# Moving half of one input tile to the weight ring, and one ScalarE copy ahead of a scaling

## The chip, the cores and the metric

The kernel runs on one core of one Trainium2 chip. The metric is the device time of one execution in microseconds, from the first to the last instruction of the core with what surrounds them; the profile's own span is a little shorter (131.2 us of an execution of 132.94 us). Before the change the median of three runs is 132.91 us (132.47 to 132.97).

## The reference

Two stages are computed. The first is a state-space scan over 4 batches x 8 heads, sequence 768, head size 32, state size 16. With `cum` the running sum of log a inside a chunk:

```
L   = exp(cum_i - cum_j), kept where i >= j
y   = ((C B^T) * L) x  +  (C state) * exp(cum_i)
state = exp(cum_last) * state + sum_j B_j x_j exp(cum_last - cum_j)
```

The second is a bilinear feed-forward layer over the 3072 tokens with 256 features: `out = ((y w_a) * (y w_b)) w_out`, with 1536 inner features. All inputs and the output are float32; the kernel multiplies in float16.

## The kernel before, in words

**Tiling.** The sequence is cut into 6 blocks of 128 steps, and two batches are worked on together. A "pair" p is one block of two batches, so there are 12 pairs. Each pair has three input tiles, B (`bn`), C (`cn`) and x (`xn`), and each tile is loaded in two halves, one for each batch (`bt` 0 and 1): `load1(eng, p, which, bt)`, with which = 0 for B, 1 for C, 2 for x. A half of B or C is 64 KB in runs of 128 bytes, a half of x 128 KB.

**Queues.** The engine named in `load1` issues the transfer: SyncE, ScalarE or GpSimd. Each issuer has a queue of its own (q1 SyncE, q10 ScalarE, q0 GpSimd) and the 16 DMA engines serve all of them. GpSimd's queue also carries the weights, converted to float16 on the way: `load_w(0)` and `load_w(1)` bring the first and second halves of w_a and w_b (`Wa`, `Wb`), `load_wo` brings w_out.

**Stages of a pair.** `scale_bc` multiplies B and C by the decay factors and gives `bm` and `cm` (L259). `transposes` turns these on PE (L286); copies bring them to `bt` (ScalarE, L297) and `ct` (DVE, L298). `scores` multiplies them on PE into the PSUM tiles SC0 and SC1 (L320). `mask` multiplies the scores with the causal mask (L354, DVE); with `by_pool=True`, ScalarE first copies the scores from PSUM to `tmp` (L351) and GpSimd multiplies (L352). `scale_x` scales x to float16 (`X16`, L243 on ScalarE). `pv_u` (L363) multiplies the masked scores with X16; the result goes to `X2T` (L451 on ScalarE, L453 on DVE for pair 0). `unit(p, k2)` is a piece of the feed-forward layer: the matmuls `aps` with Wa and `bps` with Wb (L504), a copy of `aps` on ScalarE (L518) and the product on DVE (L525). `out_mm` multiplies with w_out (L538).

**Order.** The order on each engine is written out by hand, and the engines run their own lists in that order, waiting on semaphores. Around the change it is: the loads and GpSimd's constants; pair 0 up to X2T, with `warmup` matmuls (L193) that only keep PE busy; then pair 1's C and B scaled (`scale_bc(1, 1, nc.vector)` on DVE and `scale_bc(1, 0, nc.gpsimd)`), its transposes, the first matmuls with Wa, the scores of pair 1, and so on. On DVE, `cm` of pair 1 stands ahead of the scan of block 2, of one of the four X2T evacuations of pair 0, and of the copy of the transposed C. Pair 2's x is made to wait for the second half of Wb. From pair 4 on, the transposes are done by DMA.

Of the kernel before, what the change touches and what calls it, by code (L numbers as in the profile page):

```python
# [22 lines left out]
def kernel(  # L23
# [13 lines left out]
    nc = tc.nc  # L37
# [85 lines left out]
    def load1(eng, p, which, bt, i0=0, n=64):  # L123
        blk, bp = divmod(p, NBP)
        src = (B, C, x)[which][2 * bp + bt, :, blk * Q + 2 * i0 : blk * Q + 2 * i0 + 2 * n, :]
        return eng.dma_start(  # L126
            pair_in[p][which][64 * bt + i0 : 64 * bt + i0 + n].rearrange("i h r n -> i h (r n)"),
            src.rearrange("h (i r) n -> i h (r n)", r=2),
        )
# [5 lines left out]
    def load_w(half):  # L135
        c = slice(half * KC, (half + 1) * KC)
        return [
            nc.gpsimd.dma_start(W[half], src.rearrange("(f p) e -> p f e", p=128)[:, :, c])
            for W, src in ((Wa, moe_w_a), (Wb, moe_w_b))
        ]  # L140
# [17 lines left out]
    load1(nc.scalar, 0, 2, 1)  # L158
    load1(nc.sync, 0, 2, 0)
    load1(nc.sync, 1, 0, 0)  # L160
    load1(nc.sync, 1, 1, 1)
    nc.sync.dma_start(c32, p32_t.ap())
    nc.vector.memset(warm.bitcast(u32), 0)  # L163
    nc.vector.memset(zero, 0.0)
# [19 lines left out]
        )  # L184
    load1(nc.gpsimd, 1, 0, 1)
    load1(nc.gpsimd, 1, 1, 0)
    load_w(0)
    for bt in range(2):
        load1(nc.gpsimd, 1, 2, bt)

    def warmup(n, bank, cols=512):
        for _ in range(n):
            nc.tensor.matmul(  # L193
                bank[:, 0:cols], warm[:, 0:128], warm[:, 0:cols], start=True, stop=True, skip_group_check=True
            )
# [42 lines left out]
    def scale_x(p, eng):  # L238
        X16 = mid.tile([128, H, 2, D], f16, name="x16", tag="x16")
        xo, xi = X16.rearrange("p h r d -> p (h r d)"), pair_in[p][2].rearrange("p h r d -> p (h r d)")  # L240
        st.setdefault(p, {})["X16"] = X16
        if eng is nc.scalar:
            nc.scalar.mul(xo, xi, XS)  # L243
        else:
            eng.tensor_scalar(xo, xi, XS, None, ALU.mult)  # L245
# [66 lines left out]
    def scores(p):  # L312
        BT, CT = st[p]["BT"], st[p]["CT"]
        for e in range(2):
            for r in range(2):
                for m in range(4):
                    for bt in range(2):
                        rows = slice(32 * m, 32 * m + 32)
                        c0 = (e * 2 + r) * Q
                        nc.tensor.matmul(  # L320
                            SC[m][64 * bt : 64 * bt + 64, c0 : c0 + Q],
                            BT[rows, e, r, bt],
                            CT[rows, bt],
                            start=True,
                            stop=True,
                            skip_group_check=True,
                            tile_position=(32 * m, 64 * bt),
                        )
        st[p]["T1"] = mid.tile([128, H, 2, Q], f16, name="t1", tag="t1")
# [8 lines left out]
    def product0(m2, e):  # L338

        return (  # L340
            st[0]["T1"][:, 4 * m2 : 4 * m2 + 4].rearrange("p (m e) r q -> p e m (r q)", e=2)[:, e],
            (SC0, SC1)[m2][:, :, e * 256 : e * 256 + 256],
        )

    def mask(out_in, by_pool=False, ri=False):
        o_, i_ = out_in
        c_ = causal_ri.rearrange("p r s i -> p (r s i)") if ri else causal.rearrange("p r q -> p (r q)")
        c_ = c_.unsqueeze(1).broadcast_to((128, 2, 2 * Q))
        if by_pool:
            tmp = mid.tile([128, 2, 2 * Q], f32, name="tmp", tag="tmp")  # L350
            nc.scalar.copy(tmp, i_)  # L351
            nc.gpsimd.tensor_tensor(out=o_, in0=tmp, in1=c_, op=ALU.mult)  # L352
        else:
            nc.vector.tensor_tensor(out=o_, in0=i_, in1=c_, op=ALU.mult)  # L354
# [237 lines left out]
    warmup(1, SC[3])  # L592
    warmup(2, SC[3], 128)
    scores(0)
    scale_x(0, nc.scalar)
    mask(product0(0, 0))
    mask(product0(0, 1))
    mask(product0(1, 1), by_pool=True)
    mask(product0(1, 0))
    warmup(3, tcp)  # L600
    scale_bc(1, 1, nc.vector)
# [202 lines left out]
```

## Time and profile before

| | before |
|---|---|
| time, median of 3 | 132.91 us |
| span of the profile | 131.2 us |
| mean granted PE clock | 0.974 |
| PE busy | 122.2 us (93%) |
| DVE busy | 88.6 us (68%) |
| ScalarE (ACT) busy | 72.6 us (55%) |
| GpSimd (POOL) busy | 55.7 us (42%) |
| chain that ended last | PE 85%, DMA 9%, the rest 6% |

The page divides the span into 40 slices and gives for each engine the busy share in tenths, and for PE the granted clock. The chain that ended last goes back from the last instruction to what released it, step by step. A group's line in the listings gives the source line, the engine, the operation, the tile written and read, and in brackets the idle time just ahead of it with its releaser. The DMA listing counts packets and bytes by queue.

### The profile page before, as it was taken

The page shows a single profiled execution, that of the slowest core. Times are in us where ns is not written, and L with a number is a line of the kernel's source. Part 1 is how long each engine was busy: PE and PEld are TensorE (multiplying, and loading weights), DVE is VectorE, ACT ScalarE, POOL GpSimd, SP SyncE. Part 2 cuts the span into 40 slices and gives each one's busy share as a digit, 9 for nine tenths or more (in the row PEclk, how much of TensorE's full clock was granted, in tenths as well). Part 3 has the DMA queues.
Part 4 walks back from the last instruction along what each step waited for, and adds up shares of the span by engine and source line. Part 5 has one row for each costly group of instructions (what it writes and reads, how often), then busy time and mean ns, then how long its engine had stood idle before and what let it go on. Part 6 is the DMA issues. An engine that isn't in the chain of part 4 may idle for free.

```text
span 131.2 us, 4785 instructions
## 1 busy us (share of the span) xinstructions
PE 122.2 (93%) x1964; PEld 102.5 (78%) x1964; DVE 88.6 (68%) x165; ACT 72.6 (55%) x144; POOL 55.7 (42%) x99
## 2 busy tenths in 40 slices
PE   6972599999999999999999999999999999999990
PEld 2531368898889898888888988988988888899990
DVE  2570657698597895894995985967957929925450
ACT  1460372579455647657548647566476576485530
POOL 7959049575975092290650923806437000000000
PEclk9999559999999999999999999999999999999999
DMA  3999948996314546634775566465565011110112
GB/s 71 169 159 222 168 93 162 173 202 111 84 50 90 95 127 116 168 73 66 179 70 95 157 110 140 105 102 146 97 127 143 5 45 40 40 40 5 40 40 80
DMA packets 45989, 13.79 MB, mean 105 GB/s; under 512 B 41008, under 2 KB 45776, under 8 KB 45968
## 3 DMA queue, kind: packets, MB, share of 16 engines
q1 hardware_dynamic: 42048, 10.12, 37.4%
q0 software_dynamic: 1920, 3.02, 13.4%
q10 hardware_dynamic: 2000, 0.36, 1.5%
q8 instruction: 15, 0.25, 0.8%
q14 instruction: 6, 0.05, 0.1%
HBM read 11.13 MB, written 3.15 MB: 109 GB/s over the span
## 4 chain that ended last, share of the span: by engine, by line
PE 85%; DMA 9%; ACT 1%; ACTq 1%; DVE 0%; issue 0%; DVEq 0%
PE aps L504 26%; PE ops L538 24%; PE bps L504 24%; DMA cn<-in_C_dram 9%; PE SC L320 3%; PE SC L363 3%; PE SC L380 1%; PE SC L425 1%; PE fps L221 1%; PE ops L759 1%; ACT bt L297 1%; ACTq L126 1%; PE SC L286 0%; ACT asb L518 0%; PE SC L397 0%; DVE cm L259 0%
## 5 line engine op out<-in xcount | busy, mean ns | idle before, releaser
L525 DVE TENSOR_TENSOR hk<-bps,asb 128x512 f16<-128x512 f32 x72 | 49.2, 687 | 17.9 <-ACT asb L518 17.6
L518 ACT COPY asb<-aps 128x512 f32<-128x512 f32 x72 | 42.1, 587 | 17.8 <-PE aps L504 16.7
L504 PE MATMUL aps<-X2T,Wa 128*128 128x256 f16 x288 | 44.6, 279 | 0.0
L504 PE MATMUL bps<-X2T,Wb 128*128 128x256 f16 x288 | 43.6, 276 | 0.0
L538 PE MATMUL ops<-Wo,hk 128*128 128x256 f16 x276 | 33.9, 273 | 0.0
L504 PEld LDWEIGHTS <-Wb 128*128 128x128 f16 x288 | 30.1, 105 | 2.2
L504 PEld LDWEIGHTS <-Wa 128*128 128x128 f16 x288 | 29.1, 105 | 3.4 <-DVE X2T L453 0.3
L538 PEld LDWEIGHTS <-hk 128*128 128x128 f16 x276 | 26.0, 98 | 3.6 <-DVE hk L525 0.2
L354 DVE TENSOR_TENSOR t<-SC,causal_ri 128x512 f16<-128x512 f32 x32 | 21.1, 681 | 0.0
L251 POOL TENSOR_TENSOR planes<-cn,fC 128x256 f16<-128x256 f32 x8 | 5.0, 620 | 32.2 <-DMA cn<-in_C_dram 22.8
L553 ACT ACTIVATE osb<-ops 128x256 f32<-128x256 f32 x23 | 8.8, 384 | 16.5 <-PE ops L538 16.3
L245 POOL TENSOR_SCALAR x<-xn 128x512 f16<-128x512 f32 x9 | 13.4, 1489 | 0.8
L441 ACT ACTIVATE X2T<-SC 64x256 f16<-64x256 f32 (+1 forms) x24 | 10.9, 456 | 4.9 <-PE SC L380 3.7
L354 DVE TENSOR_TENSOR t<-SC,causal 128x512 f16<-128x512 f32 x13 | 8.4, 683 | 1.8 <-PE SC L320 1.7
L468 DVE SCALAR_TENSOR_TENSOR U<-SC,G,gU 128x64 f32<-128x64 f32 x16 | 4.3, 282 | 6.8 <-ACT X2T L441 6.3
L259 POOL TENSOR_TENSOR bm<-bn,fB 128x256 f16<-128x256 f32 x11 | 6.8, 621 | 0.6 <-PE bps L504 0.6
L352 POOL TENSOR_TENSOR t<-tmp,causal 128x512 f16<-128x512 f32 x3 | 3.5, 1155 | 7.8 <-ACT tmp L351 7.8
L193 PE MATMUL SC<-warm 128*128 128x512 f16 (+1 forms) x15 | 4.9, 473 | 1.2 <-DVE warm L163 1.2
L363 PEld LDWEIGHTS <-x 64*32 64x32 f16 x384 | 3.2, 91 | 2.6 <-issue 0.7
L193 PEld LDWEIGHTS <-warm 128*128 128x128 f16 x22 | 2.3, 124 | 3.7 <-issue 1.9
L297 ACT ACTIVATE bt<-SC,ch 128x256 f16<-128x256 f16 x6 | 2.5, 471 | 4.3 <-PE SC L286 4.2
L363 PE MATMUL SC<-t,x 64*32 64x128 f16 x352 | 4.6, 219 | 0.0
(78 smaller groups left out, 82.5 us busy)
## 6 DMA issues: line engine op xcount, KB each, us to landing
out_dram<-osb SPq DMA_DIRECT2D x23, 128.0 KB, 2.3
xn<-in_x_dram SPq DMA_DIRECT2D x21, 128.0 KB, 3.6
bn<-in_B_dram SPq DMA_DIRECT2D x20, 64.0 KB, 2.9
cn<-in_C_dram SPq DMA_DIRECT2D x19, 64.0 KB, 3.3
Wa<-in_moe_w_a_dram POOLq DMA_DIRECT2D x2, 384.0 KB, 6.0
Wb<-in_moe_w_b_dram POOLq DMA_DIRECT2D x2, 384.0 KB, 7.4
Wo<-in_moe_w_out_dram POOLq DMA_DIRECT2D x2, 384.0 KB, 7.1
xn<-in_x_dram POOLq DMA_DIRECT2D x2, 128.0 KB, 7.7
```

The costliest lines, as they stand in the source:

```text
L193: nc.tensor.matmul(bank[:, 0:cols], warm[:, 0:128], warm[:, 0:cols], start=True, stop=True, skip_group_check=True)
L245: eng.tensor_scalar(xo, xi, XS, None, ALU.mult)
L251: eng.tensor_tensor(out=planes[p % 2][:, 4:6].rearrange("p r (h n) -> p r h n", n=N), in0=pair_in[p][which].rearrange("p h r n -> p r h n" ...
L259: eng.tensor_tensor(out=m_, in0=pair_in[p][which].rearrange("p h r n -> p r h n"), in1=(f[:, blk, :, bp] if factor is None else factor).un ...
L354: nc.vector.tensor_tensor(out=o_, in0=i_, in1=c_, op=ALU.mult)
L363: nc.tensor.matmul(py[bt, u][32 * (g ^ 2 * bt) : 32 * (g ^ 2 * bt) + 32] if p >= P0 else py[bt][32 * g : 32 * g + 32, u * Q : (u + 1) * Q] ...
L441: nc.scalar.activation(out=X2T[to, p, bt].rearrange("p u (i r) -> p u r i", r=2), in_=SCt[bt][fr, :, 0:Q].rearrange("p u (r i) -> p u r i" ...
L504: nc.tensor.matmul(ps[:, kk * 2 * Q : (kk + 1) * 2 * Q], W[k // 6][:, f, k % 6 // 3 * 384 : (k % 6 // 3 + 1) * 384].rearrange("p (c kk) -> ...
L518: (nc.vector.tensor_copy if on_dve else nc.scalar.copy)(asb, a_ps)
L525: nc.vector.tensor_tensor(out=s["hk"][:, 2 * k2 : 2 * k2 + 2, :].rearrange("p k q -> p (k q)"), in0=b_ps, in1=asb, op=ALU.mult)
L538: nc.tensor.matmul(o_ps[:, 0:d_model], hk[:, k, bt * Q : (bt + 1) * Q], Wo[:, k, :], start=(k == 0), stop=(k == NK - 1), skip_group_check= ...
L553: nc.scalar.activation(out=o_sb, in_=o_ps[:, 0:d_model], func=AF.Copy, scale=1.0 / (YS * YS))
```

## The change

Two edits. The half of pair 1's C for batch half 1 is no longer issued by SyncE behind the other first loads; GpSimd issues it, behind the other half of the same tile and ahead of the first weights. And in ScalarE's order the copy of pair 0's scores for GpSimd's mask (inside `mask(..., by_pool=True)`) now stands ahead of the scaling of pair 0's x. The first is meant to let pair 1's C go through the queue in which its other half and the weights go; the second is meant to let GpSimd begin its mask sooner. Nothing else differs, and what is computed is the same.

```
@@ -158,7 +158,6 @@
     load1(nc.scalar, 0, 2, 1)
     load1(nc.sync, 0, 2, 0)
     load1(nc.sync, 1, 0, 0)
-    load1(nc.sync, 1, 1, 1)
     nc.sync.dma_start(c32, p32_t.ap())
     nc.vector.memset(warm.bitcast(u32), 0)
     nc.vector.memset(zero, 0.0)
@@ -184,6 +183,7 @@
         )
     load1(nc.gpsimd, 1, 0, 1)
     load1(nc.gpsimd, 1, 1, 0)
+    load1(nc.gpsimd, 1, 1, 1)
     load_w(0)
     for bt in range(2):
         load1(nc.gpsimd, 1, 2, bt)
@@ -592,10 +592,10 @@
     warmup(1, SC[3])
     warmup(2, SC[3], 128)
     scores(0)
-    scale_x(0, nc.scalar)
     mask(product0(0, 0))
     mask(product0(0, 1))
     mask(product0(1, 1), by_pool=True)
+    scale_x(0, nc.scalar)
     mask(product0(1, 0))
     warmup(3, tcp)
     scale_bc(1, 1, nc.vector)
```

More of the change, by code (lines that the diff above doesn't have):

```diff
@@ L160 @@
     load1(nc.sync, 1, 0, 0)
-    load1(nc.sync, 1, 1, 1)
     nc.sync.dma_start(c32, p32_t.ap())
@@ L186 @@
     load1(nc.gpsimd, 1, 1, 0)
+    load1(nc.gpsimd, 1, 1, 1)
     load_w(0)
@@ L594 @@
     scores(0)
-    scale_x(0, nc.scalar)
     mask(product0(0, 0))
@@ L598 @@
     mask(product0(1, 1), by_pool=True)
+    scale_x(0, nc.scalar)
     mask(product0(1, 0))
```

## The prediction

> **What bounds the kernel now.** I began with the page's busy shares: PE is busy 93% of the span, and the row of 40 slices shows its one weak stretch, slices 4 and 5 (13.1 to 19.7 us).
>
> ```profile
> PE   6972599999999999999999999999999999999990
> PEclk9999559999999999999999999999999999999999
> ```
>
> The second row is the granted clock in tenths: half speed in just those two slices. Behind them PE is busy in every slice but the last, so what is won before 20 us should reach the end. Then the chain that ended last, up to 23 us (start, length, what):
>
> ```profile
> 4.66 9.24 DMA cn<-in_C_dram
> 13.90 0.03 issue
> 13.93 0.02 DVEq L259
> 13.95 0.04 issue
> 13.99 0.44 DVE cm L259
> 14.43 0.04 issue
> 14.47 0.39 PE SC L286 x2
> 14.87 0.43 PE tc L193
> 15.29 1.71 PE aps L504 x8
> 17.00 0.58 PE SC L320 x24
> 17.58 0.97 PE aps L504 x4
> 18.55 1.99 PE bps L504 x12
> 20.54 0.83 PE fps L221 x24
> 21.36 0.35 PE SC L363 x32
> ```
>
> For 9.24 us the chain is one transfer: 64 KB of pair 1's C (`load1(nc.sync, 1, 1, 1)`), issued at 4.66 and landed at 13.90. DVE's scaling of that tile (`cm`, L259) waits, and on DVE behind it stand `scan(2, 3)`, the last quarter of X2T of pair 0 (L453) and the copy of the transposed C (L298). So PE has neither C to transpose nor a complete X2T for the first weight matmul. DVE and PE in order of time (last bracket: idle time and its releaser):
>
> ```profile
> 7.44 1.97 DVE L354 TENSOR_TENSOR t<-SC,causal 128x512 f16<-128x512 f32 x3 [0.32 <-PE SC L320]
> 13.99 0.43 DVE L259 TENSOR_TENSOR cm<-cn,fC 128x256 f16<-128x256 f32 x1 [4.59 <-DMA cn<-in_C_dram]
> 10.62 0.28 PE L286 MATMUL SC<-ident,bm 128*128 128x128 f16 x2
> 14.47 0.39 PE L286 MATMUL SC<-ident,cm 128*128 128x128 f16 x2 [3.57 <-DVE cm L259]
> ```
>
> DVE is free from 9.41, PE from 10.90. Why is 64 KB so slow? The queues from 8 to 13 us (packets, MB, share of 16 engines):
>
> ```profile
> q0 software_dynamic: 604, 1.00, 105.2%
> q1 hardware_dynamic: 567, 0.08, 14.7%
> ```
>
> q0 holds GpSimd's transfers, q1 SyncE's. Both send about as many packets, but those of q0 carry 1.7 KB on average and those of q1 0.14 KB: the C half crawls between the weights.
>
> **What the Trainium skill says.** (1) "DMA: Bandwidth & Descriptors", section "Queues, rings and completion order": each DMA engine goes round the queue rows that have work, one packet per turn. The two counts above agree. (2) The same page, "SWDGE vs HWDGE vs iDMA": a packet of GpSimd's queue gathers descriptors, up to 4096 B by preference. The trace agrees: between 4.5 and 5.0 us, while B half 1 of pair 1 goes through it, q0 sent 0.06 MB in 19 packets, not in 512 runs of 128 B. So the same 64 KB is about one packet per engine in the weight ring. (3) "TensorE: Matmul & The Clock Gate", "What's actually happening": the clock is halved after an idle window of about 3.4 us and restored after a busy one. PE idles 10.90 to 14.47, the clock is half from 12.95 to about 19.7, and the 128x256 matmuls take 421 ns at the most in place of 273. I take from it that without the 3.57 us hole it stays up.
>
> **The change part by part.**
>
> *The transfer moved.* SyncE loses one issue (0.60 us at 4.66); its constants follow sooner; nothing waits for that. GpSimd gets one issue: the two beside it take 0.71 and 0.92 us, I take 0.71. Its queue behind: Wa, Wb, two x loads, ending at 7.35, so now at 8.06. GpSimd then idled until 8.83, so no compute is late by this, but the transfers start 0.71 later.
>
> *When does C land now?* The C half ahead of it in the ring was issued at 3.79 and landed 4.3 later, 8.1. One place behind: 8.1 + 0.71 = 8.8. Bounds: 8.3 if the issue alone counts, 9.6 if the whole landing time slips by another packet and its receipt. DVE is busy until 9.41 anyway; I take "no wait", at most 0.2.
>
> *When does Wa land?* The first Wa half has no landing time in the listing. Work it from packets: the tile has 256 row pieces (128 partitions x 2), with 16 completions 272 packets; counting q0 from 7.0 in steps of 0.5 us gives 306 by 10.0, so its data were through at 9.75. Wb, 544 packets, was through at about 11.75 and its landing is recorded at 5.18 + 7.7 = 12.9, 1.15 later. So Wa landed near 10.9. New: 10.9 + 0.71 = 11.6. Low end 11.2 (SyncE's competing runs are gone), high end 12.1 (the added packet counts on top). Likewise Wb 12.9 to 13.6 and the second x half of pair 1, 6.65 + 7.7 = 14.3, to 15.0.
>
> *The order on ScalarE.* Now: `scale_x` waits 0.56 for x, runs from 7.58, the copy (tmp, L351) only from 8.11, and GpSimd's mask (1.15) from 8.83 to 9.98. The scores end at 7.31, so after: tmp about 7.4 to 7.97, mask at 8.06 (behind its issues), done 9.2; x16 from 8.0 to 8.63. PE's first y matmuls move from 8.26 to about 8.7, yet all but two of them wait for DVE's second mask (8.78), so nothing is lost. The second group (10.04 in the trace) then waits for DVE's third mask at 9.41 and goes at about 9.5: half a microsecond won, `bm` and the Wa/Wb issues of the second half go with it (10.51 to about 9.9). I book it at zero, as Wa comes later than all of this.
>
> *The new start of the weights.* DVE: masks to 9.41, cm 0.43, scan 0.33, X2T 0.25: 10.5. PE transposes C near 10.0. X2T is complete at 10.5, Wa at 11.6: the wait for C gives way to a shorter one for Wa. First `aps` at 11.6 in place of 15.09: 3.5 us. PE then idles about 10.8 to 11.6 alone, and I expect full clock.
>
> *From there to `unit(1, 0)`* (aps at 22.60 in the chain, so 7.5 us after 15.09). At full clock: 8 aps at 0.109 apart = 0.9 (12.5), scores 0.4 (12.9), then DVE: two masks 1.3, reciprocal and selector 0.75, third mask 0.65: 15.7. The other branches: Wb at 13.6 and 12 bps 1.3 give 14.9; x at 15.0 and its scaling 0.65 give 15.65. Three branches meet at 15.7: y and state matmuls 0.35 + 0.35, factors 0.55, two semaphore hops 0.3: `aps` of pair 1 at about 17.3. In place of 7.5 us it is 5.7. Sum: 3.5 + 1.8 = 5.3 us.
>
> *Is it kept?* The second weight half: (0, 3) starts at 25.77, then at 20.5; its Wb landed at 11.26 + 7.1 = 18.4, and with 0.7 for the later ring at 19.1: kept. SyncE's loads of pairs 2 to 4 wait for that Wb and do not come 5 us sooner. Pair 3's C landed at 28.0; used at 33.5, then 28.2: just enough. Pair 3's x landed at 31.1, wanted by GpSimd at 29.5 (34.8 now): GpSimd may lag by up to 1.5. But the transposed planes of pair 4 land at 41.7 for scores at 44.70, a slack of 3.0. Hidden, and I take off 0.3 for small waits. 132.9 - 5.3 + 0.3 = 127.9.
>
> **The rivals.**
> (a) *The clock still falls.* For it: even now a window with 1.9 us of work (12.95 to 16.4) did not raise it. Against: the window after 9.55 would hold about 2.4 us of 3.4, and that before it held as much and kept the clock. Then only the shift of the start is left: 132.9 - 3.5 = 129.4.
> (b) *Given back later.* Loads of pairs 3 and 4 come at the old times and PE waits for them in the 20s and 30s. If 3 of the 5.3 us go: 130.5. Against: the slacks above.
> (c) *The wait is the same in another place*: the C half in the new ring, or Wa, lands only at 13.5 to 14.5: time within 0.5% of 132.9, say 132.5. For it: the ring is the busiest one. Against: the half ahead landed at 8.1.
> (d) *Slower.* If the ring went on only after the new transfer had landed, Wa would slip by its 4.3 us and the issue by 0.71: 10.9 + 5.0 = 15.9, past 15.09 by 0.8: 133.7. Against: the weights' packets ran from 7.0 on, though the C half before them landed at 8.1.
>
> **How the numbers follow.** Forecast 0.66 (127.9), (a) 0.14, (b) 0.11, (c) 0.05, (d) 0.04. The landing of Wa (11.2 to 12.1) moves the forecast by -0.4 and +0.5, the unbooked half microsecond and the kept slack by as much again downward: 127.0 to 128.9. The range goes on to take in (a) and ends short of (b): 127.0 to 129.9. Faster: 0.66 + 0.14 + 0.11 = 0.91; same 0.05; slower 0.04.
>
> **What would show it.** In the new profile: C's scaling on DVE right behind the third mask, at 9.4 to 9.8; the chain of waits with Wa in the place of the C half; GpSimd's mask at about 8.1; first `aps` at 11.2 to 12.1; no 5 in the clock row; pair 1's first `aps` at 17 to 18; no PE wait over 0.3 us behind 20 us. It would be wrong if a landing on GpSimd's ring took longer than I counted, or if a half-speed slice stayed.

## The result, and the profile after

The changed kernel takes 127.26 us (median of 4 runs, 127.23 to 127.39), the kernel before 132.89 (median of 4, 132.47 to 132.97). The ratio is 0.9584, 95% interval 0.9563 to 0.9605: 5.6 us, where 5.0 were forecast. The span went from 131.2 to 125.5 us.

In later runs the kernel before mostly has a mean granted clock of 0.974, sometimes near 0.986, and in one of 59 runs 1.0, with 128.24 us; so that this single run does not stand for the kernel before, the experiments below are compared by the medians of all runs, with their ranges, and by the runs at full clock where some had lost it.

The two rows of the page that showed the weak stretch, now:

```profile
PE   6979999999999999999999999999999999999990
PEclk9999999999999999999999999999999999999999
```

The half-speed slices are gone, and PE's busy share no longer dips behind the third slice. The chain that ended last, in the same stretch (start, length, what; short pieces of "issue" left out):

```profile
2.93 0.86 POOL bn L126
3.79 1.39 POOL cn L126 x2
5.18 0.68 POOL Wa L138
5.86 7.10 DMA Wb<-in_moe_w_b_dram
13.01 1.49 PE bps L504 x12
14.59 0.90 PE fps L221 x24
15.49 0.35 PE SC L363 x32
15.84 0.31 PE SC L380 x32
16.14 0.59 PE fps L221 x16
16.73 0.55 PE aps L504 x4
```

The C half is no longer in it. What stands there is GpSimd issuing one transfer after another and then the flight of Wb, for which PE waits at 13.01, but only for 0.15 us. Pair 1's first `aps` begins at 16.73 in place of 22.60: at that point 5.9 us are won. DVE and PE in order of time:

```profile
7.53 1.89 DVE L354 TENSOR_TENSOR t<-SC,causal 128x512 f16<-128x512 f32 x3 [0.32 <-PE SC L320]
9.34 0.41 DVE L259 TENSOR_TENSOR cm<-cn,fC 128x256 f16<-128x256 f32 x1
10.28 0.28 PE L286 MATMUL SC<-ident,bm 128*128 128x128 f16 x2
10.40 0.28 PE L286 MATMUL SC<-ident,cm 128*128 128x128 f16 x2
10.52 0.38 PE L193 MATMUL tc<-warm 128*128 128x512 f16 x1
10.89 1.05 PE L504 MATMUL aps<-X2T,Wa 128*128 128x256 f16 x8
```

The scaling of C has no bracket any more: it follows the third mask without a wait. The two transposes that stood 3.85 us apart are 0.12 apart, and the first `aps` begins at 10.89, 4.2 us earlier, and takes 1.05 us for eight in place of 1.91.

### The profile page after: what moved, and what is told of

The parts are those of the page before. It is cut to its first block, busy times and chain, and to the rows that moved or that the text cites. A ratio compares the mean times of both kernels' runs of the same rounds, so it can differ in the third digit from the quotient of the medians.

```text
span 125.5 us, 4786 instructions
## 1 busy us (share of the span) xinstructions
PE 119.9 (96%) x1964; PEld 101.3 (81%) x1964; DVE 88.8 (71%) x165; ACT 72.5 (58%) x144; POOL 56.6 (45%) x100
## 4 chain that ended last, share of the span: by engine, by line
PE 84%; DMA 6%; POOL 4%; DVE 2%; ACT 1%; issue 1%; ACTq 0%; POOLq 0%
PE aps L504 25%; PE bps L504 24%; PE ops L538 23%; DMA Wb<-in_moe_w_b_dram 6%; PE SC L320 3%; PE SC L363 3%; DVE t L354 2%; PE SC L380 1%; PE SC L425 1%; PE fps L221 1%; POOL cn L126 1%; PE ops L759 1%; POOL bn L126 1%; ACT bt L297 1%; POOL causal L181 1%
## 5 line engine op out<-in xcount | busy, mean ns | idle before, releaser
L504 PE MATMUL aps<-X2T,Wa 128*128 128x256 f16 x288 | 43.3, 273 | 0.0
L504 PE MATMUL bps<-X2T,Wb 128*128 128x256 f16 x288 | 42.9, 273 | 0.2 <-DMA Wb<-in_moe_w_b_dram 0.2
L504 PEld LDWEIGHTS <-Wb 128*128 128x128 f16 x288 | 29.6, 103 | 2.2 <-DMA Wb<-in_moe_w_b_dram 0.4
L504 PEld LDWEIGHTS <-Wa 128*128 128x128 f16 x288 | 28.5, 103 | 3.0 <-DMA Wa<-in_moe_w_a_dram 0.3
L441 ACT ACTIVATE X2T<-SC 64x256 f16<-64x256 f32 (+1 forms) x24 | 10.9, 456 | 4.9 <-PE SC L380 3.8
L269 POOL COPY planes<-bm 128x128 f16<-128x128 f16 x16 | 4.2, 291 | 0.5
## 6 DMA issues: line engine op xcount, KB each, us to landing
out_dram<-osb SPq DMA_DIRECT2D x23, 128.0 KB, 2.5
xn<-in_x_dram SPq DMA_DIRECT2D x21, 128.0 KB, 3.8
```

The costliest lines, as they stand in the source:

```text
L441: nc.scalar.activation(out=X2T[to, p, bt].rearrange("p u (i r) -> p u r i", r=2), in_=SCt[bt][fr, :, 0:Q].rearrange("p u (r i) -> p u r i" ...
L504: nc.tensor.matmul(ps[:, kk * 2 * Q : (kk + 1) * 2 * Q], W[k // 6][:, f, k % 6 // 3 * 384 : (k % 6 // 3 + 1) * 384].rearrange("p (c kk) -> ...
```

## The experiments

Twelve experiments follow, on nine kernels and, twice more, the changed one; one of the nine stands there twice. Each is compared with runs made beside it on the same chip, unless the text says otherwise. A granted clock written as full is one of 0.995 or more.

**1. Each edit alone.** First the C half moved, with ScalarE in its old order:

```
     load1(nc.gpsimd, 1, 1, 0)
+    load1(nc.gpsimd, 1, 1, 1)
     load_w(0)
...
     scores(0)
     scale_x(0, nc.scalar)
```

> The C half of pair 1 in the weight ring; ScalarE keeps its old order (x of pair 0 scaled first). Theory A (the forecast: the copy's place is hidden behind the landing of Wa): 127.3 us as with both edits, first aps at 10.9. Rival B (Wa landed at 10.85, earlier than worked out, so the half microsecond of the mask is on the path): the second group of y goes at 10.0 in place of 9.6, the last quarter of X2T is written at about 10.9, first aps at 11.2, time 127.5 to 127.7.

127.72 us (127.60 to 128.85), with first `aps` at 11.34 in the profile. Because the changed kernel was not run beside it on this chip, the same kernel ran a second time where it was:

> The C half moved, ScalarE in its old order, once more beside the changed kernel on one chip. The run before put the copy's place at 0.4: first aps at 11.3, 0.3 to 0.5 above the changed kernel. If it was the chip: the same time.

127.85 (127.48 to 129.16) against 127.09 (126.98 to 127.19) for the changed kernel. At full clock alone the two groups are 127.5 to 128.0 and 127.0 to 127.2: the copy's place is worth half a microsecond or a little more (0.7 between these medians) once C is out of the way. Rival B held in its time, but the traces show another way to it than the one it named. In the first of the two profiles the mask on GpSimd began at 8.84 in place of 8.26, and

```profile
9.33 0.94 DVE L259 TENSOR_TENSOR cm<-cn,fC 128x256 f16<-128x256 f32 x1
10.20 0.83 DVE L200 TENSOR_TENSOR_SCAN Pr<-a_sb,zero 32x128 f32<-32x128 f32 x1
10.96 0.25 DVE L453 TENSOR_SCALAR X2T<-py 128x128 f16<-128x128 f32 x1
```

DVE's scaling of C took 0.94 us where the changed kernel's took 0.41: here it began while GpSimd's mask ran, there as that mask ended. The second group of y was done by about 10.35, when ScalarE took its last quarter of X2T (10.41; 10.10 in the changed kernel); DVE's quarter came only at 10.96, in place of 10.43, since DVE was held up by its own scaling and scan. That this X2T then sets the start is inferred. In this profile Wa also landed late, at 5.15 + 6.2 = 11.35, just behind the end of X2T (11.21); in the second one Wa was there at 10.65 and X2T at 11.34, but the clock had halved, and `aps` began at 11.78, behind slower transposes and a filler.

Then the copy alone, with C left in SyncE's queue:

> Only ScalarE's copy moved ahead; the C half stays in SyncE's queue. Theory A (the C half alone sets the path): C still lands at about 13.9, first aps at 15.1, 132.9 us, no difference. Rival B (the mask's place is on the path by itself): 132.4 us.

132.22 (129.53 to 133.33) against 132.41 (128.24 to 133.75) before: no difference that these runs can tell. In the trace DVE's `cm` still waits 4.7 us for C, until 14.59. The second edit paid only when the first had cleared the path. (This trace warns of the clock row: it has full speed throughout, yet the 128x256 matmuls with Wa from 15.69 on take up to 421 ns, as at half speed before. So the row can miss a fall.)

**2. What the clock alone is worth.** The kernel before, with matmuls on zeros (fillers) in the hole:

```
-    transposes(1, apart=True)
+    transposes(1, between=lambda: warmup(15, tcp), apart=True)
```

> The kernel before, with 15 matmuls on zeros (128x512, 3.2 us in all) between PE's transposes of pair 1's B and C, so that PE is busy while it waits for the C half; nothing else changes. Theory A (the halved clock cost 1.8 us by itself, beside the late start): first aps still at 15.1, no half-speed slice, aps of pair 1 at about 20.8 in place of 22.6, time 131.1. Rival B (that stretch waits for Wb, for x and for DVE, so the clock costs little): aps of pair 1 at 22.3 or later, time 132.6 to 132.9.

130.97 (130.48 to 132.86) against 132.41: 1.4 us. Six of its 22 runs still lost the clock (0.986 or 0.987) and took 132.2 to 132.9; the others took 130.5 to 131.1. The profiled run has a mean clock of 0.997; its C half landed at 4.76 + 9.10 = 13.86, and still:

```profile
10.79 3.40 PE L193 MATMUL tc<-warm 128*128 128x512 f16 x15
14.43 0.28 PE L286 MATMUL SC<-ident,cm 128*128 128x128 f16 x2 [0.23 <-DVE cm L259]
14.77 1.11 PE L504 MATMUL aps<-X2T,Wa 128*128 128x256 f16 x8
```

Pair 1's first `aps` came at 20.58 in place of 22.54, of which 0.3 is the start (14.77 for 15.09) and 1.6 the faster stretch. The wait and the clock are two costs of the same late transfer, and they can be taken apart. (The one run of the kernel before at full clock, 128.24 us, is 2.2 us faster than the best of these, so more than the clock must have been different in it. It left no trace, and what it was stays open.)

**3. Place in the ring, or size of the packets?** Two kernels move the C half elsewhere. The first puts it into the weight ring, but behind the weights:

```
-    load1(nc.gpsimd, 1, 1, 1)
     load_w(0)
+    load1(nc.gpsimd, 1, 1, 1)
```

> Both edits, but the C half stands in the weight ring behind Wa and Wb in place of ahead of them. Theory A (the ring is worked off in order, so what counts is the place ahead of the weights): C lands at 13.0 to 13.6, near the 13.9 of before, first aps at 14.3 to 14.8, the clock falls again, time 132.0 to 132.7. Rival B (any place in the ring will do, as its packets are large): C lands at 9 to 10, time 127.3.

132.25 (130.99 to 133.08): no gain against 132.41. Wa landed at 4.49 + 6.5 = 10.99, Wb at 5.20 + 8.3 = 13.5, and C, issued at 5.91, took 8.0 us and landed at 13.9, as late as in SyncE's queue. The transfers of the ring landed in the order of their issue, so "ahead of the first weights" is the half of the edit that counts. The second gives C a queue with no B ahead of it, ScalarE's:

```
     load1(nc.scalar, 0, 2, 1)
+    load1(nc.scalar, 1, 1, 1)
...
-    load1(nc.gpsimd, 1, 1, 1)
```

> Both edits, but ScalarE issues the C half, behind the x half of pair 0, so it is in a queue of its own with small packets and not in the weight ring. Theory A (packets: 128-byte runs get one turn for each large packet of the weights, in whatever small-packet queue they stand): C lands at 12 to 14, first aps at 13.5 to 15, time 131.3 to 132.6. Rival B (place: in SyncE's queue it only stood behind 64 KB of pair 1's B): C lands at 8 to 9.6, time 127.3 to 127.8.

132.81 (131.91 to 133.52) against 132.64 (131.63 to 135.27): no gain. C took 9.57 us and landed at 14.35. The queues from 8 to 13 us of this run (packets, MB, share of 16 engines):

```profile
q0 software_dynamic: 623, 1.02, 103.9%
q10 hardware_dynamic: 519, 0.06, 13.1%
```

It is the picture of the kernel before with the queue's name exchanged: 519 packets of 0.12 KB, nearly the whole C half with its 512 runs, go between 623 of the weights. What stood ahead in this queue, the x half of pair 0, had landed at 3.4 + 4.3 = 7.7, and C took 6.6 us more. So it was not the place behind pair 1's B, and not SyncE: in both queues of small packets C waited while the weights ran. The Trainium skill, "DMA: Bandwidth & Descriptors", section "Queues, rings and completion order", says that a DMA engine takes turns between its queues packet by packet. The traces agree in that the small packets get through a few at a time, but not at one for one: from 10 to 12 us they were 138 beside 278 of the weights here, and 140 beside 269 in the kernel before.

**4. What bounds the start now.** One more half tile ahead of the weights, B's, taken from SyncE:

```
-    load1(nc.sync, 1, 0, 0)
...
     load1(nc.gpsimd, 1, 1, 1)
+    load1(nc.gpsimd, 1, 0, 0)
     load_w(0)
```

> The changed kernel with one more transfer ahead of the weights: SyncE's half of pair 1's B goes to GpSimd's ring as well. Theory A (what starts PE now is the landing of Wa, and of Wb after it, which the issue delays by 0.7): first aps at 11.5, bps at 13.6, time 0.6 above the changed kernel on the same chip. Rival B (X2T and C set the start at 10.7, Wa is hidden): within 0.2 of the changed kernel.

128.06 (127.77 to 128.89) against 127.65 (127.17 to 130.47) for the changed kernel beside it, first `aps` at 11.39; at full clock 127.8 to 128.3 against 127.2 to 127.9. This run does not tell A from B: the longer list of issues also moved GpSimd's mask to 8.79, and with it the end of X2T to 11.16, while Wa landed at 5.84 + 5.5 = 11.34. So a kernel that leaves GpSimd's list as long as it was:

```
+    load1(nc.gpsimd, 1, 2, 0)
     load_w(0)
-    for bt in range(2):
-        load1(nc.gpsimd, 1, 2, bt)
+    load1(nc.gpsimd, 1, 2, 1)
```

> The changed kernel with one half of pair 1's x (128 KB) moved ahead of the weights in GpSimd's ring: GpSimd's list is as long as before up to its mask, C and X2T are not touched, only Wa and Wb come later, by 0.77 of issue or a little more. Theory A (Wa starts PE): first aps at 11.6 to 11.9, bps 0.8 later too, time 0.6 to 0.9 above the changed kernel. Rival B (X2T sets the start): first aps at 10.9, time within 0.3.

X2T was complete at 10.63, C's transposes began at 10.18, and

```profile
12.03 1.54 PE L504 MATMUL aps<-X2T,Wa 128*128 128x256 f16 x8 [1.35 <-DMA Wa<-in_moe_w_a_dram]
```

Wa, issued at 5.82, landed at 12.02, and PE waited 1.35 us for it: theory A. 128.44 (127.44 to 129.33) against 127.09; at full clock 127.4 to 127.7, so 0.35 to 0.65, a little under the forecast. In the other half of its runs, the profiled one among them, the clock fell, and they took 129.2 to 129.3. So both costs, the wait and the clock, can come back with the order of the transfers.

**5. Faster still?** The selector of the later blocks ahead of the masks on DVE:

```
     scan(3, NBLK)
+    over_mid(1, NBLK)
+    sel_over_mid(1, NBLK, nc.vector)
...
-    over_mid(1, NBLK)
-    sel_over_mid(1, NBLK, nc.vector)
     mask(product(1, 2))
```

> The changed kernel with DVE's reciprocal and selector of the later blocks ahead of pair 1's first two masks. Theory A (from the first aps on PE is nearly packed and waits only for Wb, so there is little left): factors at 14.5 in place of 14.6, time 0.1 to 0.2 below the changed kernel. Rival B (the masks on DVE set the path, and are now later): 0.3 above it.

127.38 (126.94 to 127.89), against this kernel as it is:

> The changed kernel once more, on the same chip as the others of this call, to compare tenths with. 127.3 us; first aps at 10.9.

127.65 (127.17 to 130.47). At full clock the first takes 126.9 to 127.9 and this one 127.2 to 127.9. Not told apart. In the profiled run Wa happened to land at 11.46 and Wb at 13.78, and PE waited 0.65 and 0.36 for them, so that the selector, now early, was not what anything waited for. Last, GpSimd's first issues, the weights among them, 1.2 us earlier, by building its causal mask behind them, together with the selector:

```
+    load1(nc.gpsimd, 1, 0, 1)
+    load1(nc.gpsimd, 1, 1, 0)
+    load1(nc.gpsimd, 1, 1, 1)
+    load_w(0)
     nc.gpsimd.memset(causal, 1.0)
...
-    load1(nc.gpsimd, 1, 0, 1)
-    load1(nc.gpsimd, 1, 1, 0)
-    load1(nc.gpsimd, 1, 1, 1)
-    load_w(0)
```

> The changed kernel with GpSimd's causal mask built behind the first weights' issues in place of ahead of them (1.2 us earlier issues), and the selector first as in the run before. Theory A (PE's start waits for X2T at 10.7 and for Wa, whichever is later; bps for Wb): Wa at about 9.7, Wb at 11.8, first aps at 10.7, bps without a wait, time 0.3 to 0.6 below the changed kernel. Rival B (the earlier large packets take the DMA engines from pair 0's first loads, 2.5 to 6.5 us): pair 0's scores and x come later by up to 0.9, time equal or above by up to 0.7.

128.45 (127.14 to 129.56), against the changed kernel on that chip:

> The changed kernel, beside the three others: 127.2 to 127.4 where the clock stays full, first aps at 10.6 to 10.9.

127.09 (126.98 to 127.19). Rival B, so far as a kernel with runs so far apart can say: the ring's packets now ran while pair 0's own inputs were on the way,

```profile
6.26 0.42 DVE L259 TENSOR_TENSOR cm<-cn,fps 128x256 f16<-128x256 f32 x1 [0.83 <-DMA cn<-in_C_dram]
11.21 0.62 POOL L259 TENSOR_TENSOR bm<-bn,fB 128x256 f16<-128x256 f32 x1 [1.03 <-DMA bn<-in_B_dram]
```

and pair 0's C was scaled 0.7 us later (at 5.52 in the kernel beside it), with what follows on it. The second line is the same trouble once more: pair 1's B, still in SyncE's queue, took 7.2 us to land, GpSimd waited for it, and the first `aps` began only at 12.34. This also speaks to a rival that section 3 left open, that the C half was slow there only because it was issued just behind Wa (4.7 or 4.8 against 4.5): this B was issued at 3.81, ahead of Wa, and was slow all the same, where in the changed kernel, run again, it took 4.5. And the weights gained nothing: issued at 3.96, Wa landed at 3.96 + 6.8 = 10.76, against 5.15 + 5.3 = 10.45 in the kernel beside it. No tried version beats the change.

## Why the prediction was right, by its own steps

*What bounds the kernel* held: moving the C half, and nothing else, brought 4.7 us on one chip (132.41 to 127.72) and 4.2 of 5.0 on another (132.05 to 127.85, and 127.09 with both edits). The *reason* given, small packets beside the large ones of the weights, was tested by the two other places and stands. By the queues' totals on the two pages, the move took 528 packets from SyncE's queue and added 32 to GpSimd's, so "about one packet per engine" was right. But the two counts in the prediction, 604 and 567, are no sign of turns one for one: 567 is little more than the C half itself, whatever its pace, and the pace was about one to two (section 3 of the experiments).

*C without a wait*: right. It was issued at about 4.5, took 4.3 (8.8, as worked out), and the scaling ran at 9.34, as soon as DVE was free.

*When does Wa land* was the term that was mis-sized. The forecast let it slip by the whole added issue, from 10.9 to 11.6. It landed at 5.15 + 5.7 = 10.85, below even the low end of 11.2, Wb at 12.96 (13.6 forecast; 12.9 before), and the last x half at 14.2 (15.0; 14.3 before): issued 0.7 later, landed when they had before. The reason that the prediction gave for its low end, that SyncE's competing runs are gone, does not explain it. The queues from 8 to 13 us, first of the changed kernel, then of the one with C behind the weights, where the weights were issued as early as before and SyncE's queue is quiet too:

```profile
q0 software_dynamic: 622, 1.02, 113.3%
q1 hardware_dynamic: 3, 0.00, 0.1%
```

```profile
q0 software_dynamic: 619, 1.03, 113.7%
q1 hardware_dynamic: 23, 0.00, 0.9%
```

Against 604 with 567 small packets between them, the ring got hardly more through, and with the early issue and the quiet queue together Wa still landed at 10.99. The last kernel of the experiments adds that an issue 1.2 us earlier did not help either (10.76). So for issues between 3.96 and 5.15 the landing did not follow the issue; it stayed within the spread of 10.4 to 11.5 that the runs show anyway. A likely reason, not tested by itself: in the kernels before, after, and with C behind the weights, GpSimd's queue sends 4 to 24 packets in each half microsecond from 5.0 to 7.5, while the other two still work on the first loads, and over 50 only from 7.5 or 8 on, whether the weights were issued at 4.5 or at 5.15. Issued at 5.8, with one more transfer ahead, Wa landed at 11.34 in one kernel and at 12.02 in the other, later than in any other run. The start is therefore 4.2 us earlier, where 3.5 were booked.

*From the first `aps` to pair 1's*: 5.7 us forecast from 7.5; by the timeline it is 16.66 - 10.89 = 5.8, from 7.45. The filler experiment shows that the clock accounts for 1.6 of it by itself.

*The order on ScalarE*, booked at zero "as Wa comes later than all of this": this failed with the step above. Wa came at 10.85 and X2T at 10.68, so an X2T half a microsecond later would have been the last to come, and the first experiment measured a loss of that size. How it comes about was missed: the prediction had the y matmuls wait for the mask, and the larger part is DVE's scaling and scan, slowed beside GpSimd.

*Is it kept?* Yes: PE shows no wait over 0.2 us behind 17 us. Between pair 1's `aps` (5.9 us won) and the end (5.7) 0.2 are lost, perhaps around pair 2's masks, where the chain now runs through DVE for 1.9 us. The 0.3 taken off was about right.

*Rival (a), the clock still falls*, was given 0.14 and 129.4 us. It was not seen in the four runs of the result, but of twelve later runs of the same kernel two had a mean clock of 0.987 and 0.973, with 128.91 and 130.47 us. With the four, that is two of sixteen, close to the 0.14. So "without the 3.57 us hole it stays up" held in most runs, and the hole is not the whole rule (see the last section). Rivals (c) and (d) did not come: C was there at 8.8 and Wa at 10.85.

Together: 4.2 us of start (3.5 forecast) and 1.7 of the stretch (1.8), less 0.2 (0.3), give 5.7 where 5.0 were forecast; the runs give 5.6. The mechanism was right and the miss is in the main Wa's landing.

## What to carry to other kernels

A small strided load that shares the DMA engines with bulk weights was slow by its small packets, in either of the queues tried; in the queue of the bulk, and ahead of it, it took 4.3 us in place of 9.2, and the bulk landed no later. When a wait is removed, ask what else ends within half a microsecond of it: the second edit was worth nothing alone and half a microsecond behind the first. A hole in PE can cost twice, once as waiting and once in the clock of the work that follows. A landing that is expected to follow its issue should be looked up in a run where only the issue moved.

## What the runs showed that was not expected

*The clock can fall without an idle stretch of 3.4 us.* The Trainium skill, "TensorE: Matmul & The Clock Gate", section "What's actually happening", puts the fall after an idle window of about 3.4 us. In the kernel before PE did idle for 3.57, though the fall at 12.95 came after only 2.05 of it. And in the run with x ahead of the weights PE's longest idle time was 1.35 us, and the clock was half from 12.45 to 15.85. Counting 3.4 us back from each fall, PE had been busy 2.04 of 3.41 us there, 1.81 of 3.41 in the second run of the C half alone (fall at about 10.8) and 1.04 of 3.40 in the kernel before. In that kernel the stretch before, with 2.69 of 3.40, kept the clock, and the one behind the fall, with 1.89 of 3.41, did not bring it back. So here stretches that were busy for 53 to 60% lost it and one of 79% did not. In the three profiles of the changed kernel no stretch of 3.41 us, begun every 0.4 us from 5.6 to 12.4, is busy for less than 2.65, and the clock stays up. Where between 60 and 79% the line lies is not shown. The lengths between fall and rise, 3.4 and 6.8 us, agree with the skill's window.

*DVE and GpSimd slow each other.* The scaling of C takes 0.43 us in the kernel before, with GpSimd at rest, and 0.94 to 1.05 where it begins while GpSimd's mask runs; the scan takes 0.40 there, and 0.83 where it begins while GpSimd's `bm` runs. It goes the other way too: in the changed kernel the scaling began at 9.34, just before `bm`, and kept its 0.41, while `bm` took 0.85 in place of 0.61. DVE's masks, which read one input from PSUM, keep their 0.65. The Trainium skill, "GPSIMD Engine Reference", section "1. Specifications", names contention with DVE instructions that have two SBUF inputs; the scaling and the scan are of this kind, and the traces agree.

*The landing of the same transfer varies.* Between runs of kernels with the same list of first issues Wa took 5.3 to 6.3 us, and with it the first `aps` moved from 10.6 to 11.5. This is as large as the effects looked for in the last experiments, so a difference of tenths can be told only from several runs on one chip, and one profile does not show it.
